# The last attention outputs and the first expert's rows in a new order, in a fused WKV attention and mixture-of-experts kernel

## The chip, the cores and the metric

One NeuronCore of one Trainium2 chip. The metric is the device time of one execution in microseconds; of several runs the median. The engines are called PE (TensorE, matmuls), PEld (its weight loads), DVE (VectorE), ACT (ScalarE), POOL (GpSimd) and SP (SyncE, which here only issues DMAs). Each runs its own list of instructions in order and waits on semaphores for the others.

## The reference

Two stages. The first is a linear attention with decay, batch 4, 8 heads, 768 steps, head size 48, all in float32:

```python
for t in range(S):
    cur = einsum('bhd,bhe->bhde', u * k[t], v[t])
    y[t] = einsum('bhd,bhde->bhe', r[t], state + cur)
    state = w[t][..., None] * state + einsum('bhd,bhe->bhde', k[t], v[t])
```

The second takes the 3072 resulting tokens (384 wide, all heads side by side) through a mixture of 8 experts, one per token, chosen by the largest of 8 logits:

```python
logits = x @ w_gate                       # 384 x 8
e = argmax(logits); gate = softmax(logits)[e]
out = gate * (relu(x @ w1[e]) @ w2[e])    # 384 -> 1024 -> 384
```

## The kernel before

Attention (function `attention`) runs over 32 pieces `i`: a unit is a pair of heads of one batch element, and each unit has two halves of 384 steps, cut into six chunks of 64. For each piece TensorE turns the inputs, forms the scores inside the chunks (`sc`), the chunk states (`kv`) and the output, which is the sum of two groups of products in one PSUM bank: `y_inter` (the state before the chunk, needs the scan `states` of VectorE) and `y_intra` (the scores times v). `y_out` copies the finished sum to the token rows `xr`. The output of piece `i` is made three iterations later, in iteration `i + 3`; the last three pieces are finished in the last iteration and behind the loop (lines 942 to 954, `i = NI`). Behind the loop `y_inter` of the last two pieces comes first, then `fence` (two tiny matmuls with a ScalarE copy between them, which keep the two groups of products apart on TensorE), then `y_intra`. PSUM tile `both`, also called `pair`, is two banks wide; its halves go by the tags `ps` and `pp`. `py` is another tile of two banks.

Routing of a batch element of 768 tokens: `route_x` turns the rows block by block (six blocks of 128), `route_l` forms the logits, `route_t` turns them back, `route_g` (VectorE, first operation `lg`) finds the expert, the gate weight and the prefix counts, `route_p` ends in `slu`, the place of each token, and `route_s` lets GpSimd scatter one block of rows into the DRAM buffer `xs`, which has a region for each expert. For the last batch element this is done in two halves of three blocks, `st[0]` and `st[1]` (lines 955 to 981), each with three scatters. Behind the last scatter VectorE's copy `spaced` waits for GpSimd.

The filler. Expert 0's first 192 rows (`EARLY`) are known early. `early_load` loads them during the last batch element and appends to the list `filler` small pieces of their work in plain float32: 2 x `xtr` (turn the rows), 24 x `mm1` (8 blocks f of the hidden layer, 3 products each, a relu at the third, which runs on ScalarE for f in `EA` and else on VectorE), 24 x `mm2` (3 output blocks d, 8 products each, a ScalarE copy to `ey` at the eighth) and 2 x `otr` (turn the result, scale it on VectorE to `eo`, scatter it by GpSimd with `otail`). `fill(n)` emits the next n of them; how many stand where is written by hand in `FILL`.

After attention, expert 0's weights are split into a high and a low part in a reduced-precision format (`W[0][2](g, ...)`, ScalarE writes H, VectorE writes L; g = 0, 1 are w1, 2, 3 are w2), with the rest of the filler between the splits. Then `moe` begins: `first_load` loads the other 256 rows of expert 0 (its late rows) from `xs` and their tags (gate weight and token number), `first_turn` turns them on TensorE and splits them into `xH` and `xL`. Each expert then runs `mm1` (8 groups f of nine matmuls over four PSUM banks; each group gives hH on ScalarE and hL on VectorE, so that the fifth group needs the first one's hL) and `mm2` or `mm2d`. SyncE issues, in program order: the late rows, their tags, register loads, `zrow` (clearing rows behind the next expert's region in `xs`), the next expert's rows, tags and four weight pieces (`wstage`). Memory of `moe`'s tiles is taken over from the pools of routing (`rstk`), tile by tile as their readers are done.

Of the kernel before, what the change touches and what calls it, by code (L numbers as in the profile page):

```python
# [9 lines left out]
F32 = mybir.dt.float32  # L10
# [4 lines left out]
AF = mybir.ActivationFunctionType  # L15
# [5 lines left out]
CAP = 448  # L21
# [5 lines left out]
FILL = ((0, 0, 0, 0), 0, 1, 0, 1, 7, 8, 0, 0, (99, 99, 20, 0), (0, 2, 0, 6), (0, 0, 0, 0))  # L27
# [16 lines left out]
def wkv_moe(ctx: ExitStack, tc: tile.TileContext, r, k, v, w, u, w_gate, w1, w2, out):  # L44
# [295 lines left out]
    def attention():  # L340
        NI = 2 * NP * B
        with ExitStack() as a:
# [240 lines left out]
            def y_inter(i):  # L583
                un, h, b, pr = where(i)
                p = T["py", i]
                opened = set()
                for q in range(NB):
                    for side, par in ((0, 1), (1, 1), (0, 0), (1, 0)):
                        kr, _ = rows(side)
                        c = 2 * q + par  # L590
                        if h == 0 and c == 0:
                            continue
                        nc.tensor.matmul(p[side][64 * par:64 * par + 64, q, :], RF[i % 6][kr, c, :C],  # L593
                                         T["TT", un][kr, :, h * NCH + c], start=(side, par) not in opened, stop=False)
                        opened.add((side, par))

            def fence():
                for last in (False, True):
                    p = bank("px")[:, :1]
                    nc.tensor.matmul(p, ones, ones[:, :1], start=True, stop=True)  # L600
                    if not last:
                        nc.scalar.activation(wk.tile([P, 1], F32, name="seen"), p, AF.Copy)

            def y_intra(i, qs=range(NB)):
                un, h, b, pr = where(i)
                p = T["py", i]
                for q in qs:
                    for side, par in ((0, 0), (0, 1), (1, 0), (1, 1)):
                        ts = half(side, par)
                        nc.tensor.matmul(p[side][64 * par:64 * par + 64, q, :], SCT[i % 4][ts, side * NB + q, :],  # L610
                                         vat(un, side, par, h * NB + q),
                                         start=False, stop=q == NB - 1)
# [332 lines left out]
            fill(FILL[1])  # L945
            y_new(i - 2)
            y_inter(i - 2)
            y_new(i - 1, ("ps", "pp"))
            y_inter(i - 1)
            fence()  # L950
            y_intra(i - 2)
            y_out(i - 2)
            y_intra(i - 1)
# [3 lines left out]
            for q in range(NB + 1):  # L957
                route_x(st[q // NB], q, tags[q % 3], q in XV)
            route_l(st[0], 0, "py")
            route_x(st[1], NB + 1, tags[(NB + 1) % 3], NB + 1 in XV)  # L960
            route_t(st[0], "ps")
# [6 lines left out]
            for f in ops:  # L968
                f()
            for q in ALLQ[:NB]:  # L970
                route_s(st[0], q, scat)
# [100 lines left out]
    filler = []  # L1072

    def fill(n):
        for _ in range(min(n, len(filler))):
            filler.pop(0)()

    def early_load():
# [35 lines left out]
        def otr(bi):  # L1114
            q, n = eblocks[bi]
            p = bank("pt" if bi % 2 else "pw")[:, :DM]
            for d in range(KD):
                nc.tensor.transpose(p[:n, d * P:(d + 1) * P], yT[d][:, q:q + n], ident)
            o = ep.tile([P, DM], F32, name="eo", bufs=2)
            nc.vector.tensor_scalar(o[:n], p[:n], rows[:n, bi, DM:DM + 1], None, op0=OP.mult)  # L1120
            otail(o, n, rows[:n, bi, DM + 1:DM + 2])
# [18 lines left out]
    for g in range(4):  # L1140
        fill(len(filler) - FILL[9][g])
        W[0][2](g, "HL" if g < 2 else "H")
    fill(len(filler))
    rstk.close()

    def moe():
        with ExitStack() as a:
# [52 lines left out]
            def first_load():  # L1200
                nb = len(blocks(0))
                rows = X["rows"] = (rp.tile([P, TOPB, XG], F32, name="xT").rearrange("p q x -> p (q x)")[:, :nb * ROW]
                                    .rearrange("p (b x) -> p b x", b=nb))
                for bi, (q, n) in enumerate(blocks(0)):
                    nc.sync.dma_start(rows[:n, bi, :], xs[q:q + n])
                tags(0, EARLY)
                xalloc(0)

            def first_turn(bi):
                q, n = blocks(0)[bi]  # L1210
                q -= EARLY
                p = bank("px" if bi % 2 else "pp")[:, :DM].rearrange("p (c t) -> p c t", c=KD)
                for c in range(KD):
                    nc.tensor.transpose(p[:, c, :n], X["rows"][:n, bi, c * P:(c + 1) * P], ident[:n, :n])
                hh = X["H", 0][:, :, q:q + n]
                nc.scalar.activation(hh, p[:, :, :n], AF.Copy)
                nc.vector.tensor_tensor(X["L", 0][:, :, q:q + n], p[:, :, :n], hh.bitcast(F32), op=OP.subtract)
# [101 lines left out]
            first_load()  # L1319
            for bi in range(len(blocks(0))):  # L1320
                first_turn(bi)
            for g in range(2, 4):
                W[0][2](g, "L")
# [181 lines left out]
```

## Time and profile before

| | |
|---|---|
| median of 3 runs | 413.51 us (412.76 to 413.86) |
| the profiled execution | 410.57 us, of which the span is 408.9 |
| PE busy | 376.6 us, 92% |
| PEld busy | 334.7 us, 82% |
| DVE busy | 293.2 us, 72% |
| ACT busy | 213.4 us, 52% |
| POOL busy | 236.9 us, 58% |
| granted TensorE clock, mean | 0.996 of full speed |

Times in the views are counted from the start of the span. A line L1234 is line 1234 of the kernel before; "out<-in" are the tiles written and read. The idle time in square brackets is that of the engine just before the instruction, and behind the arrow what ended it.

### The profile page before, as it was taken

To read this page: it belongs to the slowest core of one execution; us is meant where nothing else is said; L and a number is where in the kernel's file an instruction comes from. 1 tells how busy PE (TensorE), PEld (TensorE's weight loads), DVE (VectorE), ACT (ScalarE), POOL (GpSimd) and SP (SyncE) were. 2 spreads that over 40 slices of the span, in tenths; PEclk is the share of its full clock that TensorE was granted. 3 is DMA by queue.
4 is the path that set the end of the run, shared out by engine and by line. 5 is a ranking of instruction groups with operands and counts; after the bars stand their busy time and mean duration, and the time that the engine had idled before them with its cause. 6 is when DMAs were issued, how large, how long until landed. Compare 5 with 4: busy or idle time off the path is not lost.

```text
span 408.9 us, 13532 instructions
## 1 busy us (share of the span) xinstructions
PE 376.6 (92%) x5469; PEld 334.7 (82%) x5470; DVE 293.2 (72%) x498; ACT 213.4 (52%) x438; POOL 236.9 (58%) x417
## 2 busy tenths in 40 slices
PE   7769999989998899888997999999999999999993
PEld 4557777668777768678986889999999999999993
DVE  7787888898898876367679859568587595774520
ACT  5666567656766664354273545454454564562300
POOL 8555766669977993654010006848848568388212
PEclk9999999999999999999999999999999999999998
DMA  9999999999993742325798978756758677530101
GB/s 140 168 167 158 164 178 171 185 168 212 202 174 94 184 147 75 118 80 154 140 332 178 310 151 291 169 166 211 174 166 235 182 211 204 162 116 24 47 22 38
DMA packets 149038, 66.09 MB, mean 162 GB/s; under 512 B 127774, under 2 KB 140283, under 8 KB 148966
## 3 DMA queue, kind: packets, MB, share of 16 engines
q1 hardware_dynamic: 143030, 55.36, 61.8%
q0 software_dynamic: 4336, 9.47, 6.8%
q8 instruction: 45, 0.74, 0.8%
q10 hardware_dynamic: 1600, 0.30, 0.5%
q14 instruction: 27, 0.22, 0.2%
HBM read 49.72 MB, written 15.87 MB: 160 GB/s over the span
## 4 chain that ended last, share of the span: by engine, by line
PE 66%; DVE 14%; DMA 6%; ACT 5%; issue 3%; SPq 3%; POOL 1%; ACTq 0%; POOLq 0%; DVEq 0%
PE pw L1234 5%; PE pk L1221 5%; PE pk L1220 5%; PE pk L1222 5%; PE pt L1234 5%; PE ps L1234 5%; PE pp L1234 5%; PE both L525 4%; DVE TT L564 3%; PE py L593 3%; PE py L1221 3%; PE py L1220 3%; PE py L1222 3%; DVE F L479 2%; DVE L L471 2%
## 5 line engine op out<-in xcount | busy, mean ns | idle before, releaser
L1290 POOL DMA_INDIRECT out_dram<-yo,yi x68 | 87.0, 1280 | 69.3 <-DVE yo L1286 54.6
L1056 DVE TENSOR_TENSOR w2L<-wstage,w2H 128x1536 fp32r<-128x1536 f32 x16 | 32.8, 2060 | 6.7 <-ACT w2H L1054 6.7
L275 POOL DMA_INDIRECT xs<-xr,slu x24 | 29.1, 1214 | 14.4 <-issue 9.8
L516 POOL TENSOR_TENSOR SC<-eye,qT 128x384 f32<-128x384 f32 x32 | 26.5, 828 | 16.8 <-ACT qT L509 16.7
L1056 DVE TENSOR_TENSOR w1L<-wstage,w1H 128x1536 fp32r<-128x1536 f32 x16 | 28.0, 1757 | 8.9 <-ACT w1H L1054 8.7
L471 DVE TENSOR_TENSOR_SCAN L<-pw,stepb 112x390 f32<-112x390 f32 x31 | 29.7, 957 | 5.9 <-PE pw L450 2.7
L441 POOL TENSOR_TENSOR rk<-rT,kT 112x384 f32<-112x384 f32 x32 | 31.9, 998 | 1.6 <-ACT rT L462 1.5
L1054 ACT ACTIVATE w2H<-wstage 128x1536 fp32r<-128x1536 f32 x16 | 31.5, 1978 | 0.5 <-DMA wstage<-in_moe_w_dram 0.5
L494 POOL TENSOR_TENSOR Kd<-kT,L 112x384 f32<-112x384 f32 x32 | 30.0, 937 | 1.3 <-ACT kT L466 1.3
L479 DVE TENSOR_TENSOR_SCAN F<-pw,bfw 112x390 f32<-112x390 f32 x31 | 30.0, 968 | 0.9
L513 ACT ACTIVATE Kt<-both 128x288 f32<-128x288 f32 x32 | 13.1, 411 | 29.8 <-PE both L525 28.8
L525 PE MATMUL both<-RF,Kd 48*64 48x112 f32 x768 | 28.2, 262 | 0.3 <-issue 0.2
L1221 PE MATMUL pk<-hL,w2H 128*128 128x464 f32 (+4 forms) x80 | 28.4, 355 | 0.0
L1222 PE MATMUL pk<-hH,w2L 128*128 128x464 f32 (+4 forms) x80 | 28.3, 354 | 0.0
L1220 PE MATMUL pk<-hH,w2H 128*128 128x464 f32 (+4 forms) x80 | 28.3, 354 | 0.0
L1062 POOL DMA_INDIRECT out_dram<-orow,tag x8 | 9.3, 1161 | 30.4 <-DVE orow L1308 30.0
L529 DVE COPY_PREDICATED SC<-mask,both 128x384 f32<-128x384 uint32 x32 | 18.9, 592 | 10.3 <-POOL SC L516 8.2
L1054 ACT ACTIVATE w1H<-wstage 128x1536 fp32r<-128x1536 f32 x16 | 23.5, 1481 | 1.9 <-DMA wstage<-in_moe_w_dram 1.9
L543 PEld LDWEIGHTS py<-V,Kt 64*48 64x48 f32 x704 | 17.0, 120 | 8.8 <-ACT qT L509 4.3
L564 DVE TENSOR_TENSOR_SCAN TT<-PT,AT 112x576 f32<-112x576 f32 x16 | 22.7, 1420 | 1.4 <-ACT PT L559 1.3
L1284 DVE STREAM_TRANSPOSE yo<-yT 128x416 f32<-128x416 f32 (+2 forms) x15 | 11.7, 779 | 16.5 <-ACT yT L1269 16.2
L543 PE MATMUL py<-V,Kt 64*48 64x48 f32 x704 | 22.4, 212 | 1.0 <-ACT Kt L513 1.0
(294 smaller groups left out, 1169.5 us busy)
## 6 DMA issues: line engine op xcount, KB each, us to landing
wstage<-in_moe_w_dram SPq DMA_DIRECT2D x28, 768.0 KB, 5.2
xs<-zrow SPq DMA_DIRECT2D x7, 723.8 KB, 8.2
in_w<-in_w_dram SPq DMA_DIRECT2D x30, 144.0 KB, 4.3
in_k<-in_k_dram SPq DMA_DIRECT2D x30, 144.0 KB, 4.8
in_r<-in_r_dram SPq DMA_DIRECT2D x30, 144.0 KB, 4.7
V<-in_v_dram SPq DMA_DIRECT2D x15, 168.0 KB, 4.7
V<-in_v_dram SPq DMA_DIRECT2D x16, 144.0 KB, 4.5
xg<-xs SPq DMA_DIRECT2D x12, 156.0 KB, 3.2
```

The source lines that it names most:

```text
L471: nc.vector.tensor_tensor_scan(L[:, :0:-1], g[:, GW - 1:0:-1], stepb[:GP, :0:-1], 0.0, OP.mult, OP.max)
L479: nc.vector.tensor_tensor_scan(F, T["pw", i][:, :GW - 1], T["f", i], 0.0, OP.mult, OP.add)
L525: nc.tensor.matmul(psS[half(side, c % 2), side, c // 2, :], KDM[i % 3][kr, c, :], RF[i % 6][kr, c, :], start=True, stop=True)
L543: nc.tensor.matmul(p[64 * side:64 * side + D, par, q, :], T["Kt", i][ts, side, q, :], vat(un, side, par, h * NB + q), start=fresh, stop=fresh)
L564: nc.vector.tensor_tensor_scan(t[:GP].rearrange("p e c -> p (e c)"), PT[un % 2][:GP].rearrange("p e c -> p (e c)"), AT[un % 3][:GP].rearra ...
L1054: nc.scalar.activation(hh, sv, AF.Copy)
L1056: nc.vector.tensor_tensor(ll, sv, hh.bitcast(F32), op=OP.subtract)
L1220: nc.tensor.matmul(p, lh, rh, start=first, stop=False)
L1221: nc.tensor.matmul(p, lh, rl, start=False, stop=False)
L1222: nc.tensor.matmul(p, ll, rh, start=False, stop=last)
L1234: nc.tensor.matmul(p, ws["1" + x][:, c, sl], X[y, e][:, c, :n], start=(j == 0), stop=(j == len(terms) - 1))
L1290: d = nc.gpsimd.indirect_dma_start(out=out.rearrange("n (g x) -> (n g) x", g=XP), out_offset=bass.IndirectOffsetOnAxis(ap=X["i", e][:, q:q ...
```

## The change

Five things. (1) Behind the attention loop `y_intra` of the last two pieces comes first and opens the sums, `y_inter` closes them; the fence stands between, with one filler in it. (2) The filler is dealt out anew: none of the six that ended the last iteration, one each at four places `TAIL`, two instead of one behind the first `route_g`, five instead of seven behind the second. (3) `route_t` of the first half writes `py` instead of `ps`, and a GpSimd copy of one element of `slu` goes ahead of its scatters. (4) The late rows are loaded and turned (`late_rows`) as soon as `mm2` of the filler is done, ahead of `otr`; they lie in a buffer of the token rows' pool. `otr` only turns into PSUM (`py`, `pk` instead of `pw`, `pt`) and copies the tags; scaling and scatter come later in `first_out`. (5) ScalarE's split of the last piece of w2 comes behind `xH`, VectorE's `first_out` behind `xL` and ahead of its w2 splits.

```diff
...
-FILL = ((0, 0, 0, 0), 0, 1, 0, 1, 7, 8, 0, 0, (99, 99, 20, 0), (0, 2, 0, 6), (0, 0, 0, 0))
+FILL = ((0, 0, 0, 0), 0, 2, 0, 1, 5, 8, 0, 0, (99, 99, 20, 0), (0, 2, 0, 0), (0, 0, 0, 0))
+TAIL = (1, 1, 1, 1)
...
-            def y_inter(i):
+            def y_inter(i, last=False):
...
-                opened = set()
+                opened = {(side, par) for side in range(2) for par in range(2)} if last else set()
...
                         nc.tensor.matmul(p[side][64 * par:64 * par + 64, q, :], RF[i % 6][kr, c, :C],
-                                         T["TT", un][kr, :, h * NCH + c], start=(side, par) not in opened, stop=False)
+                                         T["TT", un][kr, :, h * NCH + c], start=(side, par) not in opened,
+                                         stop=last and q == NB - 1)
-            def fence():
-                for last in (False, True):
-                    p = bank("px")[:, :1]
-                    nc.tensor.matmul(p, ones, ones[:, :1], start=True, stop=True)
-                    if not last:
-                        nc.scalar.activation(wk.tile([P, 1], F32, name="seen"), p, AF.Copy)
-
-            def y_intra(i, qs=range(NB)):
+            def fence(last):
+                p = bank("px")[:, :1]
+                nc.tensor.matmul(p, ones, ones[:, :1], start=True, stop=True)
+                if not last:
+                    nc.scalar.activation(wk.tile([P, 1], F32, name="seen"), p, AF.Copy)
+
+            def y_intra(i, qs=range(NB), first=False):
...
                         nc.tensor.matmul(p[side][64 * par:64 * par + 64, q, :], SCT[i % 4][ts, side * NB + q, :],
                                          vat(un, side, par, h * NB + q),
-                                         start=False, stop=q == NB - 1)
+                                         start=first and q == 0, stop=not first and q == NB - 1)
...
             i = NI
             for q in range(sum(SCAT[2]), 2 * NB):
                 route_s(rst[B - 2], q, scat)
-            fill(FILL[1])
             y_new(i - 2)
-            y_inter(i - 2)
+            y_intra(i - 2, first=True)
             y_new(i - 1, ("ps", "pp"))
-            y_inter(i - 1)
-            fence()
-            y_intra(i - 2)
+            y_intra(i - 1, first=True)
+            fence(False)
+            fill(TAIL[0])
+            fence(True)
+            y_inter(i - 2, last=True)
             y_out(i - 2)
-            y_intra(i - 1)
+            y_inter(i - 1, last=True)
             y_out(i - 1)
             st = [{"xr": T["xr", B - 1], "sm": sm, "qs": ALLQ[:NB]}, {"xr": T["xr", B - 1], "sm": sm, "qs": ALLQ[NB:]}]
             tags = ("pk", "px", "pp")
             for q in range(NB + 1):
                 route_x(st[q // NB], q, tags[q % 3], q in XV)
+            fill(TAIL[1])
             route_l(st[0], 0, "py")
+            fill(TAIL[2])
             route_x(st[1], NB + 1, tags[(NB + 1) % 3], NB + 1 in XV)
-            route_t(st[0], "ps")
+            fill(TAIL[3])
+            route_t(st[0], "py")
             route_x(st[1], NB + 2, tags[(NB + 2) % 3], NB + 2 in XV)
             for f in route_g(st[0], base_x):
                 f()
...
             ops = route_p(st[0], "pk")
             for f in ops:
                 f()
+            nc.gpsimd.tensor_copy(spaced, st[0]["slu"][:1, :1])
             for q in ALLQ[:NB]:
                 route_s(st[0], q, scat)
             fill(FILL[4])
...
     X = {}
     eblocks = [(q, min(P, EARLY - q)) for q in range(0, EARLY, P)]
     filler = []
+    etag = cst.tile([P, len(eblocks), ROW - DM], F32, name="etag")
+    mblocks = [(q, min(P, CAP - q)) for q in range(EARLY, CAP, P)]
+
+    def late_rows():
+        rows = xrp.tile([P, NB, ROW], F32, name="xr")
+        for bi, (q, n) in enumerate(mblocks):
+            nc.sync.dma_start(rows[:n, bi, :], xs[q:q + n])
+        for bi, (q, n) in enumerate(mblocks):
+            p = res["x", bi] = bank("px" if bi % 2 else "pp")[:, :DM].rearrange("p (c t) -> p c t", c=KD)
+            for c in range(KD):
+                nc.tensor.transpose(p[:, c, :n], rows[:n, bi, c * P:(c + 1) * P], ident[:n, :n])
...
 
         def otr(bi):
             q, n = eblocks[bi]
-            p = bank("pt" if bi % 2 else "pw")[:, :DM]
+            p = bank("py" if bi % 2 else "pk")[:, :DM]
             for d in range(KD):
                 nc.tensor.transpose(p[:n, d * P:(d + 1) * P], yT[d][:, q:q + n], ident)
-            o = ep.tile([P, DM], F32, name="eo", bufs=2)
-            nc.vector.tensor_scalar(o[:n], p[:n], rows[:n, bi, DM:DM + 1], None, op0=OP.mult)
-            otail(o, n, rows[:n, bi, DM + 1:DM + 2])
+            nc.gpsimd.tensor_copy(etag[:n, bi], rows[:n, bi, DM:])
+            res["eo", bi] = p[:n]
...
     fill(FILL[6])
-    for g in range(4):
+    for g in range(3):
         fill(len(filler) - FILL[9][g])
         W[0][2](g, "HL" if g < 2 else "H")
+    fill(len(filler) - len(eblocks))
+    late_rows()
     fill(len(filler))
     rstk.close()
 
...
                 nc.scalar.activation(hh, src, AF.Copy)
                 nc.vector.tensor_tensor(ll, src, hh.bitcast(F32), op=OP.subtract)
 
-            def first_load():
-                nb = len(blocks(0))
-                rows = X["rows"] = (rp.tile([P, TOPB, XG], F32, name="xT").rearrange("p q x -> p (q x)")[:, :nb * ROW]
-                                    .rearrange("p (b x) -> p b x", b=nb))
-                for bi, (q, n) in enumerate(blocks(0)):
-                    nc.sync.dma_start(rows[:n, bi, :], xs[q:q + n])
-                tags(0, EARLY)
-                xalloc(0)
-
             def first_turn(bi):
                 q, n = blocks(0)[bi]
                 q -= EARLY
-                p = bank("px" if bi % 2 else "pp")[:, :DM].rearrange("p (c t) -> p c t", c=KD)
-                for c in range(KD):
-                    nc.tensor.transpose(p[:, c, :n], X["rows"][:n, bi, c * P:(c + 1) * P], ident[:n, :n])
                 hh = X["H", 0][:, :, q:q + n]
-                nc.scalar.activation(hh, p[:, :, :n], AF.Copy)
-                nc.vector.tensor_tensor(X["L", 0][:, :, q:q + n], p[:, :, :n], hh.bitcast(F32), op=OP.subtract)
+                nc.scalar.activation(hh, res["x", bi][:, :, :n], AF.Copy)
+                nc.vector.tensor_tensor(X["L", 0][:, :, q:q + n], res["x", bi][:, :, :n], hh.bitcast(F32), op=OP.subtract)
+
+            def first_out(bi):
+                q, n = eblocks[bi]
+                o = op.tile([P, DM], F32, name="orow")
+                nc.vector.tensor_scalar(o[:n], res["eo", bi], etag[:n, bi, 0:1], None, op0=OP.mult)
+                otail(o, n, etag[:n, bi, 1:2])
 
...
-            first_load()
+            tags(0, EARLY)
+            xalloc(0)
             for bi in range(len(blocks(0))):
                 first_turn(bi)
+            W[0][2](3, "H")
+            for bi in range(len(eblocks)):
+                first_out(bi)
             for g in range(2, 4):
                 W[0][2](g, "L")
             for e in range(E):
```

## Rows read from the trace of the kernel before

**Rows 1.** Windows: length, busy of PE, PEld, DVE, ACT, POOL; clock, DMA, GB/s

```profile
226.60:400.00 173.40, 173.40 (x934) 169.73 (x935) 114.06 (x145) 80.29 (x109) 98.44 (x146) 1.00 0.58 165
```

**Rows 2.** Timeline of PE: start, us, line, operation, tiles, [idle before]

```profile
219.32 0.48 PE L1234 MATMUL ps<-xH,w1H 128*128 128x464 f32 x1 [1.89 <-DVE hL L1239]
```

**Rows 3.** Chain that ended last, in order of time: start, us, what

```profile
184.04 2.68 DMA xs<-xr,slu
...
186.87 0.33 SPq L1205
...
189.89 5.86 DMA xs<-zrow
...
203.25 8.68 DMA wstage<-in_moe_w_dram
```

**Rows 4.** The same chain, around the last outputs of attention

```profile
166.96 0.56 PE py L593 x18
...
168.13 0.12 PE px L600
...
168.66 0.49 PE py L610 x24
...
169.51 0.61 PE pk L173 x3
```

**Rows 5.** Timeline of PE, end of the filler and start of expert 0

```profile
180.92 2.87 PE L1110 MATMUL pw<-eh,wstage 128*128 128x192 f32 x16 [0.42 <-ACT eh L1102]
...
189.41 0.55 PE L1118 MATMUL pw<-ident,ey 128*128 128x128 f32 x3 [0.42 <-ACT ey L1112]
...
191.63 0.39 PE L1234 MATMUL ps<-xH,w1H 128*128 128x256 f32 x1 [0.69 <-ACT xH L1216]
...
196.01 0.39 PE L1234 MATMUL ps<-xH,w1H 128*128 128x256 f32 x1
```

**Rows 6.** Timelines of ACT and DVE, last iteration of attention

```profile
163.91 0.41 ACT L623 ACTIVATE xr<-py 128x288 f32<-128x288 f32 x1
...
164.12 1.34 DVE L564 TENSOR_TENSOR_SCAN TT<-PT,AT 112x576 f32<-112x576 f32 x1
```

**Rows 7.** Windows as in rows 1, the first routing half

```profile
169.50:174.20 4.70, 4.16 (x31) 2.40 (x29) 1.12 (x2) 3.02 (x8) 1.69 (x4) 1.00 0.31 116
```

**Rows 8.** Timelines of DVE, PE and ACT, routing of the last batch element

```profile
167.00 0.36 DVE L1104 TENSOR_SCALAR eh<-pw 128x192 f32<-128x192 f32 x1 [0.62 <-PE pw L1099]
...
172.92 0.41 PE L194 MATMUL both<-ident,lT 72*128 72x72 f32 x3
...
173.69 0.49 ACT L178 ACTIVATE xT<-both 128x384 f32<-128x384 f32 x1 [0.37 <-PE both L173]
...
174.22 0.23 DVE L212 TENSOR_REDUCE lg<-both 128x24 f32<-128x72 f32 x1 [2.34 <-ACT xT L178]
...
176.71 0.16 DVE L269 SCALAR_TENSOR_TENSOR slu<-sl,mn 128x3 uint32<-128x3 f32 x1
...
179.99 0.16 DVE L269 SCALAR_TENSOR_TENSOR slu<-sl,mn 128x3 uint32<-128x3 f32 x1
```

**Rows 9.** Timeline of POOL, scatters

```profile
177.64 0.97 POOL L275 DMA_INDIRECT xs<-xr,slu  x1 [6.23 <-issue]
...
190.89 0.97 POOL L1062 DMA_INDIRECT out_dram<-eo,erows  x1 [5.49 <-DVE eo L1120]
```

**Rows 10.** Timeline of DVE, end of the filler to expert 1

```profile
189.99 0.62 DVE L1120 TENSOR_SCALAR eo<-pw,erows 128x384 f32<-128x384 f32 x1 [1.15 <-PE pw L1118]
...
192.17 3.46 DVE L1056 TENSOR_TENSOR w2L<-wstage,w2H 128x1536 fp32r<-128x1536 f32 x2
...
202.71 2.14 DVE L1190 STREAM_TRANSPOSE xT<-xg 128x1440 f32<-128x1440 f32 x1 [2.05 <-DMA tag<-xs]
```

**Rows 11.** DMA issues, 160 to 232 us: count, KB each, median us to landing

```profile
xT<-xs SPq DMA_DIRECT2D x2, 193.0 KB, 2.4
```

**Rows 12.** The chain again, SP's queue

```profile
187.83 0.38 SPq L1170
```

## The prediction

> **What bounds the kernel now.** I read the table by windows first. From 226.60 to 400 us TensorE is busy for 173.40 of 173.40 us [rows 1]: experts 1 to 7 run without a gap, so whatever moves the point at 226.6 moves the end by the same amount, and nothing later is to be had. The profiled execution took 410.57 us, 408.9 of them span. The last hole on TensorE before that point is the wait of 1.89 us at 219.32 for VectorE's hL of expert 1 [rows 2].
>
> Then I read the chain of waits, backwards from there. It does not run through TensorE, but through the loads: the last token scatter (starts at 184.04, its DMA ends 2.68 us later), SyncE's queue waking at 186.87, the clearing of rows behind expert 1 (`zrow`, 5.86 us), SyncE issuing row, tag and weight loads, and the weight load that starts at 203.25 and lands at 211.9 [rows 3]; from then on ScalarE and VectorE split w2 and VectorE works through to 226. So the quantity to follow is the start of the last scatter, T = 184.04. TensorE's own work matters while it ends before that chain. The timelines of the engines from 163 us on then show what sets T.
>
> **Part 1, the order of the last outputs.** Before, TensorE ends the last iteration with six filler products, runs the two inter sums (166.96 to 168.13, 1.17), the fence (to 168.66, 0.53) and the two intra sums (to 169.51, 0.85), and starts routing at 169.51 [rows 4]. A filler product is two matmuls of 192 columns; eight take 2.87 us, 0.36 each [rows 5]. After, the six fillers are gone from here and the intra sums go first. They overwrite `py`, so they wait for ScalarE's copy out of it, 163.91 + 0.41 = 164.32 [rows 6]; start 164.4. Add 0.85, the fence 0.53 with one filler (0.36) partly in its wait, which I count as 0.15 more, and 1.17: routing starts at 167.1. The inter sums need the state scan, which ends at 164.12 + 1.34 = 165.46 [rows 6], while TensorE comes to them at 165.9; that wait is covered by 0.4 us. Part 1 is worth -2.4.
>
> **Part 2, the first routing half.** Four of the six fillers come back as `TAIL`: one in the fence (counted), one before the logits, two before `route_t`. Those three are 1.1 us; TensorE is idle for 4.70 - 4.16 = 0.54 us of this stretch now [rows 7], and I let them fill 0.4 of it, so +0.7 (bounds: 1.1, if none falls into the gaps, and 0.55). Against that, `route_t` moves from `ps` to `py`. Today it runs at 172.92 and takes 0.41, but VectorE's `lg` starts only at 174.22, right after ScalarE's copy of the *other* half of the pair tile (173.69 + 0.49 = 174.18) [rows 8]. I read this as a wait on the shared tile `both`; with its own bank `lg` starts when `route_t` ends, 173.33 + 0.05: -0.85. Bounds: 0, if something else holds it, and -0.85; I take the latter, because the copy's end fits to 0.04 us.
>
> The Trainium skill, PSUM — Partial Sum Buffer, section "PSUM bank collisions raise a hardware error", says that two engines have to be kept apart on one bank and quadrant, two readers included, but not on different banks. By that rule the two halves, which are different banks, need no wait; the row shows one all the same, so it would come from how the program's tile is tracked, or not from the tile at all. By the rule alone the sum would lack this 0.85; that is the first rival below.
>
> `lg` of the first half: -2.4 + 0.7 - 0.85 = -2.55, at 171.7. From `lg` to `slu` VectorE needs 176.87 - 174.22 = 2.65. New in this stretch is one relu of a filler (f=3, which used to run before the tail), 0.36 us on VectorE [rows 8]; I take +0.3 as it overlaps its neighbour. `slu`: -2.25, at 174.6.
>
> **Part 3, GpSimd.** The first of the last six scatters starts at 177.64, 0.77 us after `slu` ended, though GpSimd had been idle for 6.23; a scatter that waits for an `eo` (189.99 + 0.62) starts at 190.89, 0.28 after it [rows 9, 10]. The change puts a one-element copy that waits for `slu` ahead. The trace has no such pair; bounds: 0.5 gained if the wait becomes 0.28, 0.2 lost if the copy only comes on top (two small things between scatters take 1.28 - 0.97 = 0.31). I take -0.2, nearer to the row of 0.28 with the copy added. T moves by -2.45, the first scatter to about 175.2. The six scatters follow each other at (184.04 - 177.64)/5 = 1.28 [rows 3, 9]; the fourth needs the second half's `slu` by 179.0. That one ends at 180.15 now [rows 8]; two fillers fewer (7 to 5) stand before its prefix product, and it starts from a `slu` 2.25 earlier, so at 177.9 at the latest. Covered by 1.1 us.
>
> **Part 4, the first expert's late rows.** The loads wait for the scatters as before, so they are issued at 186.87 - 2.45 = 184.4 and land 2.4 us later [rows 11], by 186.8 and, for the second, 187.3. TensorE has three filler products more after the routing (1.1 us), against a routing that ends about 2.7 earlier (2.25 and the shorter wait behind the fillers); so w2's filler begins at 180.92 - 1.6 and ends at 189.0 - 1.6 = 187.4 [rows 5]. The two late transposes (0.7) then run in place of the wait of 0.42 for `ey`, and the early rows' transposes (0.7, from 189.41 to 190.12) cover the wait of 0.69 for xH. Expert 0 starts at 187.4 + 1.4 = 188.8 instead of 191.63.
>
> VectorE pays for that. From 189.99 to 192.17 it runs two `eo` and two `xL` (2.18 us), then the split of w2 (3.46), then the first hL, which TensorE needs for its fifth group, at 196.01 [rows 5, 10]. All of it is still there and now begins with xL: xH of the first block is done at about 188.25, so 188.25 + 2.18 + 3.46 + 0.38 = 194.3. TensorE would be there at 188.8 + (196.01 - 191.63) = 193.2: a new wait of 1.1 us, and only -1.7 is left on TensorE. What hides the missing 0.75 is VectorE's later wait for loads (2.05 us before xT at 202.71 [rows 10]), then TensorE's 1.89 at 219.32 [rows 2]: both are set by the load chain, which moves by the whole 2.45. TensorE, 1.7 earlier, still arrives there first. The GpSimd copies of the tags (`etag`) lie where GpSimd is idle, and the two output scatters come some 0.4 earlier than now. Part 4 by itself is worth about nothing at the end: it adds slack on TensorE that this chain does not use.
>
> **Queues.** On SyncE the order stays: two row loads, the tag load, then register loads and `zrow`. It is the same wait (scatters landed), 2.45 earlier, and all behind it moves along.
>
> **Sum.** -2.4 + 0.7 - 0.85 + 0.3 - 0.2 = -2.45 at T, passed on whole. 410.57 - 2.45 = 408.1 for an execution like the profiled one. The median of the runs is 413.51, 2.9 above the profiled one; on it the same step gives **411.1**. Its own range, from the bounds of parts 2 and 3 and 0.3 for parts 1 and 2: 410.2 to 412.2.
>
> **Rivals.**
> *The bank was not the cause.* `lg` goes on ending last behind ScalarE's copy of the sixth block. That copy moves -2.4 + 0.7 = -1.7, so T moves by -1.7 + 0.3 - 0.2 = -1.6: 411.9. For it: the two halves are different regions. Against: the 0.04 us fit.
> *TensorE becomes the bound.* VectorE's new order (eo ahead of w2's split) holds the fifth group, and the loads, packed more closely with the output scatters, no longer give the slack. Then what is left is -1.7 or less, say -1.2 with the next hL late too: 412.3. For it: VectorE is busy 188 to 195 without a gap. Against: two waits for loads stand behind it.
> *SyncE waits for TensorE* (the other side). The tag tile of expert 0 is laid on memory of the routing pools, which now hold the late rows until their transposes are done. If it falls on the late rows, SyncE stands at the tag load, which is issued at 187.83 now [rows 12], until 187.4 + 0.7 = 188.1: +0.3, and the whole load chain with it, for the register loads, `zrow` and the weights are queued behind. If it falls on something that the early transposes read, the wait lasts 0.7 more, +1.0, 414.5; and as the wait is then set by TensorE, which gets here later by what parts 1 and 2 fail to bring, a missing 0.85 makes it +1.85, 415.4. It decides from the point where SyncE reaches the tag load more than 2.45 before TensorE is through. Against: the late rows take the fourth of five buffers, and the tag tile, the first of its pool, should lie at one end.
> *No effect:* the weight loads are held by the DMA engines and land when they do now: 413.5. Against: the chain shows them waiting for SyncE.
>
> **Chances.** Forecast 0.60, bank 0.12, TensorE 0.10, SyncE 0.10, no effect 0.08. What a measurement of this kernel can tell from no change is about 0.3%, 1.24 us. Faster by more (under 412.27): nearly all of the forecast (0.57), most of the bank case (0.10), half of the TensorE case (0.05): 0.72. Slower by more (over 414.75): the dearer part of the SyncE case, 0.06. Within: 0.22. The range leaves out the SyncE case, part of the one without effect, and the far end of a good forecast: 409.9 to 413.3.
>
> **What would show it.** In the trace after: routing starts at 167.1 (part 1); `lg` within 0.1 us of `route_t`'s end (part 2); first scatter about 0.5 after `slu`, last one at 181.6 (part 3); SyncE's first row load at 184.4 and `zrow` at 187.4; TensorE waiting about 1.1 us for hL at the fifth group of expert 0 (part 4); TensorE without gaps from 224.2 on. Wrong if the last scatter moves by 2.45 and the point at 226.6 does not, or if the tag load is issued over 1 us after the row loads.

## The result and the profile after

The changed kernel takes **408.86 us** (median of four runs, 408.47 to 410.05) against 413.45 (412.76 to 413.86) for the kernel before beside it: ratio 0.990, 95% interval 0.987 to 0.993. The forecast was 411.1 with a range from 409.9 to 413.3. The direction was right, the gain of 4.6 us almost twice the 2.4 on record.

The profiled execution took 410.05 us, 408.3 of them span. Set beside the 408.9 of the execution before this looks like a gain of 0.6, and that is a trap. The kernel's time swings with TensorE's granted clock, whose mean is 0.985 here and was 0.996 there, and the whole stretch up to attention's last iteration, in which the two programs are the same, is longer by 1.06 us here (its first inter product starts at 161.43 instead of 160.37). So what follows is measured **from the start of the last iteration**, and an absolute time of after is read less 1.06.

By windows, the profile after (columns as in [rows 1]; the third number from the right is the granted clock):

```profile
14.00:20.00 6.00, 6.00 (x85) 4.11 (x84) 1.13 (x2) 2.36 (x6) 2.07 (x4) 0.50 1.12 166
218.60:226.00 7.40, 7.40 (x29) 6.36 (x30) 6.91 (x19) 0.77 (x2) 0.00 (x0) 0.77 0.97 224
218.60:400.00 181.40, 181.40 (x966) 176.79 (x967) 120.81 (x163) 80.88 (x109) 97.20 (x146) 0.99 0.59 167
```

The first row shows where such time goes: for six microseconds TensorE got 0.50, the level of 1.2 GHz instead of 2.4, and was busy for all six, right behind a wait of 1.32 us for an input (`in_r`), in a part that the change does not touch. The last row answers to [rows 1]: from 218.6 on TensorE is busy without a gap, so the end is still set by the loads and by VectorE ahead of expert 1.

The chain that ended last, parts that answer to [rows 3, 4]:

```profile
168.13 0.48 PE pk L174 x3
...
182.41 2.85 DMA xs<-xr,slu
185.40 2.38 DMA xr<-xs
187.92 0.53 PE pp L1089 x3
...
191.12 3.33 DVE w2L L1062 x2
...
199.19 0.35 DVE hL L1251
199.54 1.12 SPq L1041
...
201.72 9.38 DMA wstage<-in_moe_w_dram
211.11 2.04 ACT w2H L1060
```

The chain no longer goes through the clearing (`zrow`): behind the late rows' loads it steps over to TensorE's transposes (`pp`), VectorE's split of w2 and expert 0, and comes back to SyncE only in the midst of the four weight loads, at 199.54, behind a `hL`. The last of them starts at 201.72 (200.66 on the old scale, 2.59 earlier than in [rows 3]).

TensorE, answering to [rows 2, 5]:

```profile
179.39 2.87 PE L1127 MATMUL pw<-eh,wstage 128*128 128x192 f32 x16 [0.42 <-ACT eh L1119]
...
187.92 0.52 PE L1089 MATMUL pp<-ident,xr 128*128 128x128 f32 x3 [0.46 <-DMA xr<-xs]
...
194.84 0.39 PE L1246 MATMUL ps<-xH,w1H 128*128 128x256 f32 x1 [0.85 <-DVE hL L1251]
...
218.49 0.73 PE L1246 MATMUL ps<-xH,w1H 128*128 128x464 f32 x1 [2.60 <-DVE hL L1251]
```

VectorE, answering to [rows 8, 10]:

```profile
172.24 0.23 DVE L213 TENSOR_REDUCE lg<-py 128x24 f32<-128x72 f32 x1 [0.49 <-PE py L195]
...
175.00 0.16 DVE L270 SCALAR_TENSOR_TENSOR slu<-sl,mn 128x3 uint32<-128x3 f32 x1
...
190.52 0.60 DVE L1228 TENSOR_SCALAR orow<-py,etag 64x384 f32<-64x384 f32 x1
...
191.05 3.41 DVE L1062 TENSOR_TENSOR w2L<-wstage,w2H 128x1536 fp32r<-128x1536 f32 x2
...
200.41 2.13 DVE L1208 STREAM_TRANSPOSE xT<-xg 128x1440 f32<-128x1440 f32 x1 [0.88 <-DMA xg<-xs]
```

GpSimd, answering to [rows 9]:

```profile
175.23 0.18 POOL L975 CAST spaced<-slu 1x1 f32<-1x1 uint32 x1 [2.83 <-DVE slu L270]
...
176.04 0.97 POOL L276 DMA_INDIRECT xs<-xr,slu  x1 [0.60 <-issue]
...
190.88 4.44 POOL L1068 DMA_INDIRECT out_dram<-orow,etag  x1 [7.10 <-DVE orow L1228]
...
195.62 0.92 POOL L1068 DMA_INDIRECT out_dram<-orow,etag  x1 [0.24 <-DVE hL L1251]
```

One row nobody asked for: the first output scatter holds GpSimd for 4.44 us, where the same scatter took 0.97 before [rows 9]. And SyncE's queue, first after, then before (the second fence shows what [rows 3, 12] had only as a chain):

```profile
185.40 0.80 SPq L1085 DMA_DIRECT2D xr<-xs  x2
186.50 0.38 SPq L1188 DMA_DIRECT2D tag<-xs  x1
188.56 0.43 SPq L1347 DMA_DIRECT2D xs<-zrow  x1
193.66 1.97 SPq L1197 DMA_DIRECT2D xg<-xs  x4
195.82 3.15 SPq L1184 DMA_DIRECT2D tag<-xs  x4
199.23 3.61 SPq L1041 DMA_DIRECT2D wstage<-in_moe_w_dram  x4
```

```profile
189.89 0.43 SPq L1331 DMA_DIRECT2D xs<-zrow  x1
195.76 1.96 SPq L1179 DMA_DIRECT2D xg<-xs  x4
197.93 3.31 SPq L1166 DMA_DIRECT2D tag<-xs  x4
201.49 2.89 SPq L1035 DMA_DIRECT2D wstage<-in_moe_w_dram  x4
```

The clearing, from its issue to the row loads that wait for it, takes 193.66 - 188.56 = 5.10 us after and 195.76 - 189.89 = 5.87 before; the weights are issued 16.82 us behind the last scatter after (199.23 - 182.41) and 17.45 before. The forecast held this distance fixed. From the first weight issue to the start of the last weight load it is the other way round: 201.72 - 199.23 = 2.49 us after, 203.25 - 201.49 = 1.76 before. The waits of SyncE's queue from 198 to 206 us say so too (engine, line, what it waited for: us in total, times, longest); before has no such row:

```profile
SPq L1041 <- DVE hL L1251: 0.9, 2, 0.5
```

### The profile page after: what moved, and what is told of

Read it like the earlier page. It is cut to its first block, busy times and chain, and to the rows that moved or that the text cites. A ratio compares the mean times of both kernels' runs of the same rounds, so it can differ in the third digit from the quotient of the medians.

```text
span 408.3 us, 13538 instructions
## 1 busy us (share of the span) xinstructions
PE 380.8 (93%) x5470; PEld 338.2 (83%) x5470; DVE 292.7 (72%) x498; ACT 213.3 (52%) x438; POOL 239.4 (59%) x420
## 4 chain that ended last, share of the span: by engine, by line
PE 68%; DVE 14%; DMA 6%; ACT 4%; issue 3%; POOL 2%; SPq 1%; ACTq 0%; POOLq 0%; DVEq 0%
PE ps L1246 6%; PE pt L1246 6%; PE pp L1246 5%; PE pw L1246 5%; PE pk L1233 5%; PE pk L1234 5%; PE pk L1232 5%; PE both L526 4%; PE py L594 3%; PE py L1233 3%; PE py L1234 3%; PE py L1232 3%; DVE L L472 2%; DVE TT L565 2%; DMA wstage<-in_moe_w_dram 2%
## 5 line engine op out<-in xcount | busy, mean ns | idle before, releaser
L1302 POOL DMA_INDIRECT out_dram<-yo,yi x68 | 85.8, 1262 | 71.1 <-DVE yo L1298 56.4
L611 PE MATMUL py<-V,SC 64*64 64x48 f32 x720 | 21.6, 220 | 2.4 <-issue 1.9
```

What stands on the lines that cost most here:

```text
L1302: d = nc.gpsimd.indirect_dma_start(out=out.rearrange("n (g x) -> (n g) x", g=XP), out_offset=bass.IndirectOffsetOnAxis(ap=X["i", e][:, q:q ...
```

## The experiments

The first question was whether the tail's chain carries all of the gain, as forecast (T comes earlier, the rest moves along, part 4 is worth nothing), or whether part 4 carries some of its own; the second, by what.

**Both kernels again** (no edit).

> The kernel before, unchanged, to see how its executions differ. Two theories. Chain: the change moved only the load chain (its last scatter is 2.7 us earlier once the start of the kernel is set equal), and the rest of the measured 4.6 us is TensorE's clock, which the one profiled execution of before kept at 0.996 and the one of after lost twice. Then most executions of before run at 0.985 to 0.990 and take 412 to 414, and a profile of such a one shows half clock between 14 and 20 us. Rival, an odd profile: the executions of before keep the full clock and take 413 all the same, and the 410.57 of the profile is an outlier for another reason, such as later loads.

> The changed kernel, unchanged. Chain: 2.4 to 2.7 us under before where both have the same clock, and the half clock at 218 us, behind TensorE's wait of 2.60 us for hL, is there again, since the wait is part of the order. Rival: the half clock at 218 us was chance and is gone; then the gain is about 4.6.

Before: 414.13 (12 runs), ratio to itself 1.000 (0.998 to 1.003). After: 410.15 (12 runs), ratio 0.992 (0.988 to 0.995), mean clock 0.996 and span 404.5 in its profile, against 0.983 and 413.6 for before's. Beside them before took 413.76 (35 runs), so after is 3.6 us under it, between what the two theories want. Before's profile shows the half clock from 14 to 20 us again (0.52); after's does not show it at expert 1 (1.00, behind a wait of 1.35 us). Single executions of one kernel lie up to 8 us apart.

**Parts 1 to 3 alone**: `FILL`/`TAIL`, the order of the last outputs, `route_t` in `py`, and the copy; expert 0's late rows and the early rows' results stay as before.

```diff
-FILL = ((0, 0, 0, 0), 0, 1, 0, 1, 7, 8, 0, 0, (99, 99, 20, 0), (0, 2, 0, 6), (0, 0, 0, 0))
+FILL = ((0, 0, 0, 0), 0, 2, 0, 1, 5, 8, 0, 0, (99, 99, 20, 0), (0, 2, 0, 0), (0, 0, 0, 0))
+TAIL = (1, 1, 1, 1)
...
-            route_t(st[0], "ps")
+            route_t(st[0], "py")
...
+            nc.gpsimd.tensor_copy(spaced, st[0]["slu"][:1, :1])
```

> Only the new order of the last outputs, the filler dealt out anew, route_t in py and the copy ahead of the scatters; the late rows as in the kernel before. Chain: the scatters end 2.5 to 2.7 us earlier as in the changed kernel, and nearly the whole gain is here: 2.4 to 3 us under before; expert 0 starts about 1.2 us earlier only. Rival, both parts carry: about half of the gain, 1 to 2 us, because TensorE now reaches expert 0 late.

**Part 4 alone**: the rest of the diff, points (4) and (5) of the change.

```diff
+    fill(len(filler) - len(eblocks))
+    late_rows()
     fill(len(filler))
...
             for bi in range(len(blocks(0))):
                 first_turn(bi)
+            W[0][2](3, "H")
+            for bi in range(len(eblocks)):
+                first_out(bi)
```

> Only the late rows loaded and turned ahead of the early rows' results and w2's split behind xH; the tail as in the kernel before. Chain: no gain (within 0.4 us of before), since the scatters and so the loads of expert 1 stay where they are; a new wait of about 1 us for the first hL. Rival, both parts carry: 1.5 to 2.5 us under before.

Tail alone: 410.77 us, ratio 0.992 (0.989 to 0.995). Late rows alone: 411.45, ratio 0.9945 (0.992 to 0.997), a part that should have been worth nothing. From the start of the last iteration, two executions of before, three of after, one of each part (us; T is the start of the last token scatter, and the landing of the last weight load is told by the start of ScalarE's split of w2):

| | T | clearing takes | weights issued | last weight load starts | split of w2 | end |
|---|---|---|---|---|---|---|
| before | 23.67, 23.67 | 5.87, 5.89 | 41.12, 41.27 | 42.88, 43.03 | 51.59, 52.30 | 248.53, 249.11 |
| tail alone | 21.01 | 5.93 | 38.72 | 40.48 | 49.81 | 246.79 |
| late rows alone | 23.69 | 5.07 | 39.64 | 42.26 | 51.72 | 248.76 |
| after | 20.98, 21.25, 21.01 | 5.10, 5.10, 5.08 | 37.80, 37.31, 37.14 | 40.29, 39.51, 39.62 | 49.68, 47.94, 48.97 | 246.87, 244.90, 246.31 |

The two parts act at different places. The tail moves T by -2.66 and leaves the clearing alone; the late rows leave T alone, shorten the clearing by 0.8 and bring the weights' issue forward by 1.56. The other 0.8 comes behind the clearing: SyncE issues the four tag loads in 2.57 us, instead of 3.31 and 3.54 in before and 3.50 in the tail alone. Half of the 1.56 is lost again among the four issues, where SyncE's queue waits 0.6 to 1.2 us in this kernel and in the three executions of after: at the last load's start the late rows are worth 42.96 - 42.26 = 0.70 and the tail 2.48, together 3.18, and after has 42.96 - 39.81 = 3.15 (means). The load itself then takes between 8.4 and 9.5 us whatever the kernel, which covers 0.7 at the end of any one profile; in that of the late rows alone nothing is left of it.

Which row of part 4 does it? What the DMA engines moved while the clearing ran (queue, kind: packets, MB, share of 16 engines), before, tail alone, late rows alone, after, in this order:

```profile
q1 hardware_dynamic: 495, 0.74, 51.4%
q0 software_dynamic: 107, 0.29, 15.4%
```

```profile
q1 hardware_dynamic: 517, 0.74, 50.9%
q0 software_dynamic: 107, 0.29, 15.4%
```

```profile
q1 hardware_dynamic: 499, 0.74, 55.8%
```

```profile
q1 hardware_dynamic: 495, 0.74, 55.5%
```

With part 4 the 0.29 MB of the two output scatters are gone from this window. They fall beside the row and tag loads behind it (0.21 MB there in the late-rows kernel, 0.01 in the one before); that the tag loads are issued faster all the same is not explained by any run. Why the scatters come late, GpSimd's row in the late-rows kernel says:

```profile
193.88 4.43 POOL L1062 DMA_INDIRECT out_dram<-orow,etag  x1 [6.88 <-DVE orow L1222]
```

It is the hold again: the scatter is issued as VectorE begins the split of w2 (194.04, 3.41 us there), ends when the split has ended, and its bytes move only after the clearing.

**Output scatters left out** (192 output rows are not written).

```diff
-            otail(o, n, rows[:n, bi, DM + 1:DM + 2])
```

> The kernel before without the two GpSimd scatters that write the early rows' results (those 192 rows of the output are left out). Theory, collision: the late-rows part gained because its first output scatter is held up (4.43 us on GpSimd instead of 0.97) and its 0.3 MB no longer falls into the clearing of rows behind expert 1. Then here too the clearing lands 5.1 us after its issue instead of 5.9, the weights of expert 1 are issued 0.8 to 1.5 us earlier against the scatters, and the time falls by 0.8 to 1.5 us. Rival, order: the gain comes from the late rows lying ahead on TensorE and SyncE, not from the output scatters; then the clearing takes 5.9 as before and the time stays within 0.4 us.

```diff
-                otail(o, n, etag[:n, bi, 1:2])
```

> The changed kernel without the same two scatters. Collision: there they are already out of the clearing's way, so it lands after 5.0 to 5.1 us as it does with them; the tag loads of expert 1, beside which they fall now, may be issued up to 0.6 us faster; the time stays within 0.6 us of the changed kernel. Rival, order: nothing changes, within 0.3 us.

Beside these two runs before itself took 436.4 us (430.84 to 445.04), so the times, 441.61 and 442.59, decide nothing. The distances did answer: without the scatters the clearing takes 5.11 us in before and 5.14 in after, and the weights are issued 15.55 and 15.65 us behind T. SyncE's queue in after without them, where T is 189.99:

```profile
196.02 0.43 SPq L1346 DMA_DIRECT2D xs<-zrow  x1
201.16 1.97 SPq L1197 DMA_DIRECT2D xg<-xs  x4
203.33 2.07 SPq L1184 DMA_DIRECT2D tag<-xs  x4
205.64 3.49 SPq L1041 DMA_DIRECT2D wstage<-in_moe_w_dram  x4
```

The first kernel was timed again:

> Once more the kernel before without the two output scatters of the early rows (192 rows of the output left out), since the first time before itself took 430 to 445 us and the times told nothing. Collision: the clearing lands 5.1 us after its issue (5.9 with the scatters), the weights of expert 1 are issued about 15.6 us after the last scatter (17.5), and the time falls by 0.8 to 1.9 us. Order: 5.9, 17.5 and within 0.4 us of before.

411.41 us against 414.75, ratio 0.994 (0.9905 to 0.9974). SyncE's queue in it:

```profile
191.61 0.43 SPq L1330 DMA_DIRECT2D xs<-zrow  x1
196.50 1.95 SPq L1178 DMA_DIRECT2D xg<-xs  x4
198.66 2.23 SPq L1165 DMA_DIRECT2D tag<-xs  x4
201.13 3.59 SPq L1035 DMA_DIRECT2D wstage<-in_moe_w_dram  x4
```

The clearing takes 4.89, the tag loads 2.23 instead of 3.31, and the weights are issued 15.43 us behind T instead of 17.45; the last of them starts 41.58 us into the last iteration, 1.4 before its place in the kernel before, and the end is 1.6 earlier (247.19). Leaving only these scatters out of the old kernel gives it the same ratio as part 4. So the early rows' output scatters cost the chain of the kernel before over 1 us. The clearing has about half of what is gained up to the weights' issue, the tag loads the other half. And these scatters are all of what part 4 gains there: with them the old order takes 17.45 to 17.71 us from T to the weights (three executions) and the new one 15.79 to 16.82 (seven); without them the old order takes 15.43 and 15.55, the new one 15.65. That shows the cause up to the weights' issue. In time it is shown for the old order only, since the run of the new one without the scatters can't be compared.

**`route_t` back in `ps`**, in the changed kernel.

```diff
-            route_t(st[0], "py")
+            route_t(st[0], "ps")
```

> The changed kernel with route_t of the first half back in ps. If the shared pair tile is what held VectorE, lg starts right after ScalarE's copy of the sixth block ends, 0.8 to 0.9 us later than now against the start of the last iteration (11.7 instead of 10.8), and the last scatter is as much later (21.9 instead of 21.0). If the bank was not the cause: lg stays at 10.8.

One execution, of 440.7 us; timelines of TensorE, ScalarE and VectorE, a row each:

```profile
180.97 0.35 PE L195 MATMUL both<-ident,lT 72*128 72x72 f32 x3
...
181.69 0.49 ACT L179 ACTIVATE xT<-both 128x384 f32<-128x384 f32 x1 [0.35 <-PE both L174]
...
182.21 0.23 DVE L213 TENSOR_REDUCE lg<-both 128x24 f32<-128x72 f32 x1 [1.34 <-ACT xT L179]
```

`lg` starts 0.89 us after `route_t` has ended (181.32), and 0.03 after ScalarE's copy of the other half (182.18). The wait came from the shared tile. From `lg` to the last scatter it then takes 10.20 us (192.41 - 182.21), 10.17 in after, so the 0.85 goes on to T. Against the start of the last iteration it can't be read here, since TensorE got a clock of 0.69 in this routing.

**Without the copy on GpSimd**, in the changed kernel.

```diff
-            nc.gpsimd.tensor_copy(spaced, st[0]["slu"][:1, :1])
```

> The changed kernel without GpSimd's one-element copy ahead of the first half's scatters. It measured 0.88 us from slu to the first scatter with the copy, 0.77 in the kernel before. If the copy only comes on top: 0.77 again and the last scatter 0.1 us earlier. If it saves something: the gap grows over 0.88.

One execution, of 430.1 us: `slu` ends at 184.82, the first scatter starts at 185.60.

```profile
185.60 0.97 POOL L276 DMA_INDIRECT xs<-xr,slu  x1 [11.67 <-issue]
```

0.78 us without the copy; with it 176.04 - 175.16 = 0.88, and 0.77 before. The copy costs 0.1 and saves nothing.

**The output scatters ahead of xL**: what if they come too early for the hold?

```diff
+            for bi in range(len(eblocks)):
+                first_out(bi)
             for bi in range(len(blocks(0))):
                 first_turn(bi)
             W[0][2](3, "H")
-            for bi in range(len(eblocks)):
-                first_out(bi)
```

> The changed kernel with one order turned round: VectorE scales the early rows' results ahead of xL instead of behind it, so that GpSimd gets the first output scatter about 1 us earlier, before VectorE's split of w2 begins. Collision: that scatter takes about 1 us on GpSimd instead of 4.43, falls into the clearing again, the clearing takes 5.5 to 5.9 us instead of 5.1, the weights are issued 0.8 to 1.5 us later against the last scatter, and the time is 0.7 to 1.5 us over the changed kernel. Order: 5.1 stays, time within 0.5 us (xL comes up to 0.8 us later, which the load chain covers).

```profile
189.16 0.98 POOL L1068 DMA_INDIRECT out_dram<-orow,etag  x1 [6.47 <-DVE orow L1228]
190.45 4.01 POOL L1068 DMA_INDIRECT out_dram<-orow,etag  x1 [0.24 <-DVE xL L1223]
```

The first scatter now takes 0.98, beside xL; the second starts inside the split of w2 (190.25 to 193.66) and is held. 0.20 of the 0.29 MB falls into the clearing, which takes 5.42, between 5.1 and 5.9. So the clearing follows the traffic. What was expected behind it did not come: the tag loads are issued in 2.44 us, the weights 16.26 us behind T (16.06 to 16.82 in three executions of after), and the last weight load starts 39.20 us into the last iteration, earlier than in any of the three. The time, 408.95, ratio 0.989 (0.983 to 0.995), is not told apart from after's, where 0.7 to 1.5 us more was expected. So the 0.3 us that the clearing lost by these 0.20 MB can't be found again at the weights.

**More matmuls to keep TensorE's clock up**, and after once more beside it.

```diff
-WARM = (7,2,1,3,3,4,4)
+WARM = (7,2,7,3,3,4,4)
```

> The changed kernel with six more of the idle matmuls that keep TensorE busy at the start (WARM third entry 7 instead of 1), in the stretch where it waits 1.3 us for in_r. Chain and collision alike: the half clock between 14 and 20 us comes in fewer executions, the mean granted clock rises from 0.985 to over 0.99, and at 190 us per unit of clock the median falls by 1 to 2 us. If the clock falls for another reason: no change.

> The changed kernel again, as the measure for the two before it on the same chip: 3.0 to 4.5 us under before. Collision: clearing 5.1, weights issued 16.1 to 16.8 after the last scatter.

408.86 (ratio 0.989, 0.984 to 0.994) and 407.95 (0.986, 0.981 to 0.991) against 414.75: the added matmuls bring no gain that can be seen, a miss. The mean granted clock is 0.990 in both. After's clearing (5.08) and weights' issue (16.13 behind T) came as expected; its 6.8 us under before is more than the 3.0 to 4.5.

## Why the prediction was too small

- **Part 1, right.** Routing forecast at 167.1; measured 168.13 - 1.06 = 167.07.
- **Part 2, right.** `lg` starts 0.04 after `route_t` ends; the experiment with `ps` shows the 0.89 of the shared tile, forecast -0.85. The Trainium skill, PSUM — Partial Sum Buffer, section "PSUM bank collisions raise a hardware error", keeps two engines apart on one bank and quadrant but not on different banks; the runs fit that, since the wait goes with the tile, but none shows the two halves read at the same time. `slu` moved by -2.77 instead of -2.25, because the three fillers cost `route_t` 0.25 and not 0.7 (it ends at 172.20 - 1.06 = 171.14, 2.19 earlier); the 0.3 for the relu was right (2.92 from `lg` to the end of `slu`, 2.65 before).
- **Part 3, a small miss**: the copy was put at 0.2 lost; it loses 0.1. T moved by -2.4 to -2.7, forecast -2.45.
- **Queues, half right.** "All behind it moves along" belongs to part 4. The rival in which SyncE waits for TensorE did not happen: row load to clearing is 188.56 - 185.40 = 3.16 us after, 3.02 before [rows 3]. The tag load comes 1.10 us after the first row load (0.96 before), just over the mark that was set as "wrong", which was set too tight: it stands 0.30 behind the end of the second issue.
- **Part 4, the step that failed**: "the two output scatters come some 0.4 earlier than now. Part 4 by itself is worth about nothing at the end", and with it, in the queues, "all behind it moves along". TensorE's side was well read: the fifth group waits 0.85 us for hL, forecast 1.1. (The wait at expert 1, 1.89 before and 2.60 after, tells nothing: it is 2.36 in the second execution of before, 1.35 and 2.38 in two more of after.) But the scatters were looked at only as work of VectorE and GpSimd. Their 0.29 MB share the DMA engines with the clearing, which is on the chain [rows 3]. Put behind xL, the first scatter meets the split of w2, GpSimd is held 4.44 us, and the traffic leaves the clearing's window. The clearing then takes 5.10 us instead of 5.87, and the issue of the tag loads 2.60 to 3.15 instead of 3.31 and 3.54. The distance from T to the weights' issue, held fixed in the sum, shrinks by 1.2 us in the mean, and 0.7 of part 4's share is left at the last weight load. A term put at nothing was worth 1.3 ± 0.8 us in time (below).

What that is worth in time: a fit of the executions that the ratios rest on (60 of before, 21 of after, 11 or 12 of each part) on kernel and mean granted clock leaves, at equal clock and with 95% bounds, after -4.05 ± 0.6 us, tail alone -2.7 ± 0.8, late rows alone -1.3 ± 0.8, before without the scatters -1.8 ± 0.8. 2.7 + 1.3 makes 4.0: the forecast's chain, about as forecast, and a second term that it lacked. The 4.6 is also the difference of the means over these executions (413.70 and 409.12); the rest of it goes with the clock: 0.9839 in the mean for before and 0.9868 for after, at 183 us per unit of clock 0.5 us. No run shows that the change causes this difference.

**What stays open.** The traces show 3.15 us at the last weight load's start and 2.8 at the end (248.82 to 246.03, means of two and three), the times at equal clock 4.05. With loads that scatter by 1 us, so few profiles can't say whether the missing 0.9 is chance. Nor is it settled what holds SyncE among the four weight issues: the rows name `hL` in some executions and `qp` or `xT` in others of the same program or its parts, so the name may only be what ended last. Why 0.29 MB beside the clearing makes it 0.8 us longer, by shared bandwidth or by the order within the engines, was not tried. And why the tag loads behind the clearing are issued faster once the scatters come later or not at all, though nearly none of the scatters' bytes move beside them in the old order, no run shows.

## What to carry to other kernels

When a step of the chain is a transfer, list everything else that is on the DMA engines in its window, and where the change puts those transfers; a small output off the critical path can cost the chain a microsecond. When a term is "all behind it moves along", check each distance behind the step with the parts run alone. And compare executions from a mark inside the program up to which they are the same, not by spans: here the spans said 0.6 where the runs said 4.6.

## What the runs showed of the hardware

- **A scatter on GpSimd beside VectorE's split.** 0.97 became 4.44 us, about the 0.97 plus the 3.41 of the split, which reads two inputs in SBUF; beside xL, with one input in PSUM, it took 0.98. The Trainium skill, GPSIMD Engine Reference, section "1. Specifications", says that GpSimd shares its SBUF interfaces with VectorE and contends with VectorE instructions that have two SBUF inputs. The rows of after, of the late rows alone and of the scatters ahead of xL agree. The second scatter of the kernel before does not: it started with the split and took 0.92, and so in its second execution (0.92) and in the tail alone (0.93). What decides between the two was not tried.

```profile
192.17 0.92 POOL L1062 DMA_INDIRECT out_dram<-eo,erows  x1 [0.23 <-issue]
```

- **The clock.** The 60 executions of before had mean granted clocks from 0.967 to 0.997, with stretches at 0.50 early on, as from 14 to 20 us above. After the wait of 2.60 us at expert 1 the granted clock fell too: 0.77 from 218.6 to 226.0, where it was 1.00 before. It is not the change's doing alone: it fell to 0.77 or 0.78 at this place in five profiled executions, one of them the tail alone, behind waits of 1.98 to 2.65 us, and stayed at 1.00 in the second of before behind one of 2.36. From the start of the hL that ends the wait (217.80 after, 218.62 before) to the first product into `pw` (225.95 and 226.60) it was 8.15 us instead of 7.98, so it cost only some 0.2: at the full clock TensorE stood idle 0.69 and 0.35 us for VectorE in that stretch, at the lower one it did not.
